# Product 4 of the second projection by two levels of Strassen in one core's fused attention and MLP kernel

## The chip, the cores and the metric

The kernel runs on one core of a Trainium2 chip. The metric is the device time of one execution in microseconds, lower is better. All arithmetic is in fp32. Engine names in the profile: PE is TensorE's matmul, PEld its weight load, DVE is VectorE, ACT is ScalarE, POOL is GpSimd, SP is SyncE, which here only issues DMAs.

## What is computed

The inputs are q, k, v of shape (8 batches, 8 heads, 576 tokens, 64), and two weight matrices. Cut to what matters:

```python
kv  = einsum('bhsd,bhse->bhde', k, v)
out = einsum('bhsd,bhde->bhse', q, kv)
x   = (out / sqrt(mean(out*out, -1) + 1e-6) * g_norm)   # -> (4608 tokens, 512)
h   = x @ w_in                                          # (4608, 512) @ (512, 2048)
g   = maximum(0.01 * h, h)
y   = g @ w_out                                         # (4608, 2048) @ (2048, 512)
```

Nearly all of the work is in the two projections h and y.

## The kernel before

**Blocks, chunks and slots.** The 4608 tokens are nine blocks of 512. Block 0 is done with plain matmuls. Blocks 1 to 8 (`i` in the main loop) go through the 2048 hidden features in four chunks (`c`) of 512. A running chunk number is `n = (i - 1) * 4 + c`, from 0 to 31. The main loop walks each chunk in seven slots, `t` = 0 to 6; `slot = 7 * c + t` counts within a block. In each slot the code writes out, in this order, one step of h, pieces of other work, and one step of the output product y. TensorE runs its instructions in that order. VectorE and GpSimd keep the written order too from block 2 on (`pin`), so a late instruction on one of these holds up whatever is written behind it.

**Strassen, one level and two.** Both projections use the Winograd form of Strassen's scheme: seven products of half-size matrices in place of eight. The products are numbered 1 to 7. One level of it for y gives products of 256 x 256 times 256 x 256 for a chunk: four pairs of 128 x 128 weights against 256 columns each, two TensorE instructions for each pair, so 8 instructions. From block 2 on, h is done by two levels (`product_h_two`): each of its seven products is split into seven quarters, and each quarter is one 128 x 128 by 128 x 128 matmul, which is 2 instructions.

**Where the results of y go.** Products 1, 6, 7, 4 of a chunk add up in one PSUM bank, and products 5 and 3 in another; the two banks `oa` and `oc` swap roles from chunk to chunk. After each product the bank as it stands is added to one quadrant of y in SBUF: 1 goes to "11", 5 and 1+6+7 to "22", 1+6 and 5+3 to "12", and 1+6+7+4 to "21". These additions are DVE instructions of 128 x 512, or ACT copies in the first chunk of a block (`done` in `product_o`). A quadrant leaves for DRAM after the last chunk of its block.

**Product 2 already goes by two levels.** For chunks 4 to 29, class `Second` does product 2 (the g12 part) as seven quarters. Its seven quarter products sit in the fourth column of the bank that holds the second group of the h quarters (`hb` or `hd`), one in each slot of chunk n + 2, and DVE adds each to the "11" quadrant with a 128 x 128 instruction. GpSimd makes the sums that these need: of the weights once (`inner_w2`), and of g12 per chunk (`inner_g`, four operations of 128 x 128, written at `t` = 4 and 6).

**Timing of the y products.** A queue runs two slots behind (`LAG = 2`): y's products of chunk n start at `t` = 2 of chunk n + 1. With product 2 elsewhere, the order is 1, 5, 6, nothing, 7, 3, 4, so that in the steady state the slots `t` = 0 to 6 hold, behind their eight h and `Second` quarters: product 3, product 4, product 1, product 5, product 6, nothing, product 7.

**What feeds and drains h.** For `t` = 0 to 6, h runs its products 1, 2, 6, 5, 7, 3, 4. Products 1, 6, 5, 4 are copied out of PSUM by ACT (line 951), 2, 7, 3 are added by DVE. At the end of the chunk seven DVE additions of 128 x 512 put the four quadrants of g together, ACT applies the leaky ReLU (`relu`, line 832) to each, and GpSimd makes four sums of them (`sums_of`) for y's products 3, 5, 6, 7.

**Other work.** Attention for a later batch is cut in steps placed by `FINE_SLOTS` and `LATE_SLOTS`. The Winograd sums of the next block's x are made on DVE in slots 20 to 22 (`sums`, from `sides_x`), and the two-level sums on GpSimd in slots 24, 25 and after the chunk (`inner`). The weight sums for y, `t12` and `t34`, are read back from DRAM for each chunk as two loads of 512 KB (`sides_w2`, line 673). The h weights are read through a ring of five.

Of the kernel before, what the change touches and what calls it, by code (L numbers as in the profile page):

```python
# [23 lines left out]
def kernel(  # L24
# [39 lines left out]
    P = 128  # L64
# [34 lines left out]
    NW = U * NE * P  # L99
    w1_all = consts.tile([P, 2 * NC * NW], F32, name="w1_all")  # L100
    stage = consts.tile([P, 3 * NW], F32, name="stage")
    pairs = consts.tile([P, 4 * NW], F32, name="pairs")
    g_all = [consts.tile([P, 4 * U * N2], F32, name=f"g_{i}") for i in range(2)]

    def view(t, lo, *shape):
# [79 lines left out]
    zeros = view(g_all[0], 0, NT)  # L185
    nc.vector.memset(zeros[:, :64], 0.0)
    nc.vector.memset(zeros[:, 64:], 0.0)
    ident = consts.tile([P, P], F32, name="ident")

    def make_ident():  # L190
        pin(nc.gpsimd.memset(ident, 1.0))
# [448 lines left out]
    def sides_w1(c):  # L640
# [9 lines left out]
        def more():  # L650
# [5 lines left out]

    w2_dram = [[dram.tile([P, 2, U, N2], F32, name=f"w2_{c}_{i}") for i in range(2)]
               for c in range(NC)]
    t12, t34 = pair(2, 2, U, N2), pair(3, 2, U, N2)
    writes = []  # L660

    def sides_w2(n):

        c = n % NC
        b11, b12 = w2_sb[0][c][:, :, :N2], w2_sb[0][c][:, :, N2:]
        b21, b22 = w2_sb[1][c][:, :, :N2], w2_sb[1][c][:, :, N2:]

        def sums(i):  # L670
            t = (t12, t34)[i]
            if n >= NC:
                pin(nc.sync.dma_start(t, w2_dram[c][i]))
                return
            if i == 0:
                add(nc.gpsimd, t[:, 0], b12, b11, True)
                add(nc.gpsimd, t[:, 1], b22, t[:, 0], True)
            else:
                add(nc.gpsimd, t[:, 0], b22, b12, True)
                add(nc.gpsimd, t[:, 1], b21, t12[:, 1], True)  # L680
            if (n, i) == (NC - 1, 1):

# [54 lines left out]
    def read(to):  # L737
        nonlocal n_read
        while n_read < min(to, len(reads)):
# [5 lines left out]
    qc = pair(0, 4, 3, P)  # L745
    xt1 = [work.tile([P, 2, N2], F32, tag="xt1", name="xt1"),
           view(w1_all, RING * NG + 24 * P, 2, N2)]
    xt24 = [work.tile([P, 2, 2, N2], F32, tag="xt24", name="xt24"),
            view(w1_all, RING * NG + 16 * P, 2, 2, N2)]
    xi = view(stage, 0, 3, 7, P)  # L750

    def sides_x(i):


        x = xTs.pop(i)
        b11, b12 = x[:, :2, :N2], x[:, :2, N2:]
        b21, b22 = x[:, 2:, :N2], x[:, 2:, N2:]
        home = i % 2 if i > 1 else 0
        t1, t2, t4 = xt1[home], xt24[home][:, 0], xt24[home][:, 1]
        if i == 1:  # L760
            t4 = opool.tile([P, 2, N2], F32, tag="o", name="xt4", bufs=6)
        t3 = b12
        sides = {1: b11, 2: b21, 3: b22, 4: t4, 5: t1, 6: t2, 7: t3}

        def sums():
            for t, a, b in ((t1, b12, b11), (t2, b22, t1), (t3, b22, b12), (t4, b21, t2)):
                add(nc.vector, t, a, b, True)
                yield

        batches, quarters, at = [], {k: {} for k in ORDER}, 0  # L770
        upper, lower = (x[:, h:h + 2, :].rearrange("p r (t v n) -> p t r v n", t=2, v=2)
                        for h in (0, 2))
        for js, y in (((1, 7), upper), ((2, 3), lower),
                      ((6, 4), xt24[home].rearrange("p t r (v n) -> p t r v n", v=2)),
                      ((5,), t1.rearrange("p r (v n) -> p r v n", v=2).unsqueeze(1))):
            terms = [y[:, :, r, v, :] for r in range(2) for v in range(2)]
            terms += [xi[:, k, at:at + len(js), :] for k in range(3)]
            batches.append(terms)
            for n, j in enumerate(js):
                for k, term in zip((1, 7, 2, 3, 5, 6, 4), terms):  # L780
                    quarters[k][j] = term[:, n, :]
            at += len(js)

        def inner(kind):
            for y11, y12, y21, y22, t1, t2, t4 in batches:
                if kind == 0:
                    add(nc.gpsimd, t1, y12, y11, True)
# [8 lines left out]
    def strassen(tags, left, right, done, order=ORDER, pieces=None):  # L796

# [3 lines left out]
        for i in order:  # L801

            if i is None:
                yield
                continue
            b = tags[0 if i in (1, 6, 7, 4) else 1]
            if i in FRESH:
                banks[b] = ps_m.tile([P, 2, N2], F32, tag=b, name=f"{b[0]}_{b[1]}")
            bank = banks[b]
            if pieces and b == tags[0]:  # L810
                if i == 1:
                    homes = [bank] + [ps_m.tile([P, 2, N2], F32, tag=t, name=f"o_{t}")
                                      for t in ("ha", "hc")]
                    ends = [t.rearrange("p u n -> p (u n)")[:, :cols.stop - cols.start]
                            for t, (_, cols) in zip(homes, pieces)]
                for to, (part, cols) in zip(ends, pieces):
                    for r in range(2):
                        matmul(to, lhsT=left(i, part, r), rhs=right(i, part, r)[:, cols],
                               start=(i == 1 and r == 0), stop=(r == 1), skip_group_check=True)
                done(i, ends)  # L820
                yield
                continue
            for part in range(2):
                for r in range(2):
                    matmul(bank[:, part, :], lhsT=left(i, part, r), rhs=right(i, part, r),
                           start=i in FRESH and part == 0 and r == 0, stop=(r == 1),
                           skip_group_check=True)
            done(i, bank.rearrange("p u (v n) -> p (u v) n", v=2))
            yield

# [47 lines left out]

    gi = view(pairs, 12 * P, 4, P)

    def inner_w2(c):
        y = w2_sb[1][c]
# [7 lines left out]

    def inner_g(c, half):

        g = g_of(c)[3]
        a11, a21, a12, a22 = (g[:, n, :] for n in range(4))
        s1, s2, s3, s4 = (gi[:, n, :] for n in range(4))
        if half == 0:
            add(nc.gpsimd, s1, a21, a22)
            add(nc.gpsimd, s2, s1, a11, True)  # L900
# [4 lines left out]
    class Second:  # L905
# [17 lines left out]
        def done(self, k, bank):  # L923
# [2 lines left out]
            add(nc.vector, to, bank, to)  # L926
            if self.n % NC == NC - 1 and k == ORDER[-1]:
                self.finish("11", self.o)

    def product_h_two(i, c, quarters, to, second):  # L930

# [41 lines left out]
    def product_o(n, g_sides, os, finish, second):  # L973

        c = n % NC
        w_sides, _ = sides_w2(n)
        sums = sides_w2(n + 1)[1] if n + 1 < NC * (NB - 1) else lambda i: None
        if c == 0:

            for key in ("12", "22", "11", "21"):  # L980
                os[key] = opool.tile([P, 2, N2], F32, tag="o", name=f"o{key}", bufs=6)
# [6 lines left out]

        def done(i, bank):
            key, fresh = into[i]  # L990
            if isinstance(bank, list):
                for at, (end, (part, cols)) in enumerate(zip(bank, pieces)):
                    to = os[key][:, part, cols]
# [8 lines left out]
                nc.scalar.copy(to, bank)  # L1002
            else:
                add(nc.vector, to, bank, to)
            if c == NC - 1 and i in (2, 7, 3, 4):
                finish(key, os[key])

            if i == (6 if second else 5):
                sums(0)
            elif i == 4:  # L1010
                sums(1)


        yield from strassen((("oa", "oc"), ("oc", "oa"))[n % 2], lambda i, part, r: g_sides[i][:, 2 * r + part, :],
                            lambda i, part, r: w_sides[i][:, r, :], done,
                           (1, 5, 6, None, 7, 3, 4) if second else ORDER,
                           pieces=pieces)

    def go(steps, n=None):
        while n is None or n > 0:  # L1020
# [16 lines left out]
    def first_block(between):  # L1037
# [26 lines left out]
                       start=(now[2] == 0), stop=(n == 2 * NC * U))  # L1064
            between(n, 1)
        for t in range(4):
            o = opool.tile([P, DM], F32, tag="o", name="o", bufs=6)
            if t % 2:
                nc.scalar.copy(o, accs[t])
            else:  # L1070
# [37 lines left out]
    for part in range(2):  # L1108
# [4 lines left out]
    FINE_SLOTS = {1: 1, 2: 1, 4: 1, 9: 1, 10: 2, 11: 1, 12: 1, 15: 1, 16: 2, 17: 2, 18: 1, 19: 1,  # L1113
                  23: 1, 24: 1, 25: 1, 26: 1}
    LATE_SLOTS = (3, 4)

    LAG = 2

# [1 line left out]
    HELD = (22, 24, 26)  # L1120
    o_queue, waited = collections.deque(), 0

    seconds = {}

    def second_of(n):
        if n in seconds:
# [9 lines left out]
    for i in range(1, NB):  # L1136
# [4 lines left out]
        for c in range(NC):  # L1141
# [3 lines left out]
            for t in range(7):  # L1145
                slot = 7 * c + t
                go(h_steps, 1)
                if not one:

                    if t == 6:  # L1150
                        go(h_steps, 1)
                    if slot in LATE_SLOTS:
                        go(late, 1)
                    for _ in range(FINE_SLOTS.get(slot, 0)):
                        go(a_steps, 1)
                    if i + 1 < NB:
                        if slot == 20:
                            x_sides, new_quarters, sums, inner = sides_x(i + 1)
                        if slot in (20, 21, 22):
                            go(sums, 2 if slot == 20 else 1)  # L1160
                        if slot == 24:
                            inner(0)
                        elif slot == 25:
                            inner(1)
                    load_some()

# [1 line left out]
                if now - 1 in seconds:  # L1168
# [2 lines left out]
                            inner_g((now - 1) % NC, half)  # L1171
                    if t == 5 and now <= 2 * NC:
                        inner_w2((now - 1) % NC)
                if slot == 4 and not one:
                    while writes:
                        pin(nc.sync.dma_start(*writes.pop()))
# [78 lines left out]
```

## Time and profile before

| | |
|---|---|
| time, median of 3 runs | 916.78 us (916.37 to 917.01) |
| span of the profiled run | 915.5 us |
| PEld, weight loads | 775.6 us, 85% |
| DVE | 628.2 us, 69% |
| ACT | 327.6 us, 36% |
| POOL | 367.0 us, 40% |
| DMA, all queues | 200.06 MB, mean 219 GB/s |

A group in the profile is one kind of instruction; its columns are the line, the engine, the operation, output and inputs with their shapes, the count, the busy time, the mean length of one, and the idle time of the engine just ahead of it with what ended that idle time. Line 118 is the helper through which every matmul goes, and line 636 the helper of every addition, so instructions are told apart by the tiles they name: `w` is a weight of y, `pairs` a buffer of weight sums and of other sums, `gs` the sums of g, `h_ha` to `h_hd` and `o_a`, `o_c` PSUM banks. The time of an instruction in the profile contains its latency, so matmuls in a row overlap: what one costs is the distance from its start to the next start.

In the timeline, chunks of 4 x about 24 us make a block of 96.8 us: product 1 of the third chunk of a block starts at 506.03 us in one block and at 602.92 us in the next.

### The profile page before, as it was taken

The page shows a single profiled execution, that of the slowest core. Times are in us where ns is not written, and L with a number is a line of the kernel's source. Part 1 is how long each engine was busy: PE and PEld are TensorE (multiplying, and loading weights), DVE is VectorE, ACT ScalarE, POOL GpSimd, SP SyncE. Part 2 cuts the span into 40 slices and gives each one's busy share as a digit, 9 for nine tenths or more (in the row PEclk, how much of TensorE's full clock was granted, in tenths as well). Part 3 has the DMA queues.
Part 4 walks back from the last instruction along what each step waited for, and adds up shares of the span by engine and source line. Part 5 has one row for each costly group of instructions (what it writes and reads, how often), then busy time and mean ns, then how long its engine had stood idle before and what let it go on. Part 6 is the DMA issues. An engine that isn't in the chain of part 4 may idle for free.

```text
span 915.5 us, 18030 instructions
## 1 busy us (share of the span) xinstructions
PE 909.1 (99%) x6976; PEld 775.6 (85%) x6976; DVE 628.2 (69%) x1168; ACT 327.6 (36%) x645; POOL 367.0 (40%) x440
## 2 busy tenths in 40 slices
PE   8999999999999999999999999999999999999998
PEld 5444448888998999899999999999999999999997
DVE  5876985587457876587756786678659755755565
ACT  5454533242135233533343324332343333223330
POOL 2000246977633472226321642264226422642222
DMA  9999908895599678877896689658765676667632
GB/s 267 243 243 237 239 35 258 263 304 167 175 360 286 224 213 263 235 233 211 255 261 216 219 250 263 230 179 227 224 184 176 188 221 200 184 187 223 199 107 92
DMA packets 90229, 200.06 MB, mean 219 GB/s; under 512 B 9888, under 2 KB 42272, under 8 KB 90144
## 3 DMA queue, kind: packets, MB, share of 16 engines
q1 hardware_dynamic: 79680, 187.04, 69.5%
q10 hardware_dynamic: 10016, 10.69, 3.4%
q8 instruction: 56, 0.92, 0.4%
q0 software_dynamic: 448, 1.18, 0.3%
q14 instruction: 29, 0.24, 0.1%
HBM read 172.39 MB, written 26.48 MB: 217 GB/s over the span
## 4 chain that ended last, share of the span: by engine, by line
PE 95%; DMA 2%; DVE 1%; POOL 1%; issue 0%; ACT 0%; ACTq 0%; DVEq 0%; POOLq 0%
PE o_a L118 18%; PE o_c L118 18%; PE h_ha L118 11%; PE h_hb L118 11%; PE h_hc L118 8%; PE h_hd L118 8%; PE o_acc L118 6%; PE h_ps L118 6%; PE o_ps L118 3%; PE h_a L118 1%; PE h_c L118 1%; PE kv_ps L118 1%; DMA pairs<-in_v_dram 1%; PE h_b L118 1%; PE h_d L118 1%; DMA w<-pairs 1%
## 5 line engine op out<-in xcount | busy, mean ns | idle before, releaser
L636 POOL TENSOR_TENSOR gs<-g 128x512 f32<-128x512 f32 x64 | 81.7, 1277 | 253.3 <-ACT g L832 253.3
L832 ACT ACTIVATE g<-g 128x512 f32<-128x512 f32 x124 | 78.2, 631 | 130.4 <-DVE g L636 130.4
L951 ACT COPY w_all<-h_ha 128x512 f32<-128x512 f32 x84 | 48.9, 582 | 173.9 <-PE h_ha L118 160.5
L118 PE MATMUL o_a<-pairs,gs 128*128 128x256 f32 x384 | 91.3, 381 | 0.0
L118 PE MATMUL o_c<-pairs,gs 128*128 128x256 f32 x376 | 89.2, 380 | 0.0
L636 DVE TENSOR_TENSOR o<-h_hb,o 128x128 f32<-128x128 f32 x104 | 29.8, 286 | 83.3 <-ACT pairs L951 83.2
L118 PEld LDWEIGHTS o_a<-pairs,gs 128*128 128x128 f32 x384 | 69.8, 190 | 9.2 <-POOL pairs L636 1.2
L636 DVE TENSOR_TENSOR o<-o_c,o 128x512 f32<-128x512 f32 (+1 forms) x91 | 61.1, 672 | 24.1 <-PE o_c L118 23.7
L118 PEld LDWEIGHTS o_c<-pairs,gs 128*128 128x128 f32 x376 | 68.3, 190 | 7.6
L636 DVE TENSOR_TENSOR o<-o_a,o 128x512 f32<-128x512 f32 x75 | 51.2, 682 | 28.2 <-PE o_a L118 28.1
L118 PE MATMUL h_ha<-stage,w_all 128*128 128x128 f32 x448 | 59.6, 276 | 0.0
L118 PEld LDWEIGHTS h_ha<-stage,w_all 128*128 128x128 f32 x448 | 56.6, 192 | 3.0 <-issue 0.7
L118 PE MATMUL h_ps<-xT,w_all 128*128 128x512 f32 (+1 forms) x136 | 58.1, 571 | 0.3 <-DVE w_all L258 0.3
L118 PE MATMUL o_acc<-w,g 128*128 128x512 f32 x128 | 57.7, 594 | 0.0
L636 DVE TENSOR_TENSOR g<-g,pairs 128x512 f32<-128x512 f32 x84 | 55.6, 689 | 1.9
L636 POOL TENSOR_TENSOR pairs<-g 128x128 f32<-128x128 f32 x52 | 23.7, 456 | 77.3 <-PE h_hb L118 48.5
L118 PEld LDWEIGHTS h_ps<-xT,w_all 128*128 128x128 f32 x136 | 25.4, 190 | 29.0 <-issue 26.1
L118 PEld LDWEIGHTS o_acc<-w,g 128*128 128x128 f32 x128 | 24.1, 190 | 30.2 <-issue 29.9
L636 DVE TENSOR_TENSOR w_all<-h_hc,w_all 128x512 f32<-128x512 f32 x56 | 38.3, 684 | 15.9 <-PE h_hc L118 15.6
L636 DVE TENSOR_TENSOR o<-h_hd,o 128x128 f32<-128x128 f32 x78 | 22.0, 283 | 38.2 <-ACT pairs L951 38.1
L118 PE MATMUL h_hb<-stage,w_all 128*128 128x128 f32 x336 | 46.7, 275 | 0.0
L636 POOL TENSOR_TENSOR pairs<-w 128x512 f32<-128x512 f32 x4 | 5.3, 1328 | 98.7 <-ACT cut L245 98.7
(229 smaller groups left out, 2262.4 us busy)
## 6 DMA issues: line engine op xcount, KB each, us to landing
w_all<-w SPq DMA_DIRECT2D x196, 448.0 KB, 4.2
pairs<-w SPq DMA_DIRECT2D x56, 512.0 KB, 4.3
out_dram<-o ACTq DMA_DIRECT2D x35, 256.0 KB, 4.4
v_in<-in_v_dram SPq DMA_DIRECT2D x29, 288.0 KB, 5.5
k_in<-in_k_dram SPq DMA_DIRECT2D x28, 288.0 KB, 5.3
q_in<-in_q_dram SPq DMA_DIRECT2D x56, 144.0 KB, 6.0
q_in<-in_q_dram SPq DMA_DIRECT2D x56, 140.0 KB, 6.0
w<-stage SPq DMA_DIRECT2D x12, 512.0 KB, 4.8
```

Of the source, the lines that this page charges most:

```text
L118: pin(nc.tensor.matmul(*args, **kw))
L636: ins = eng.tensor_tensor(out_, a, b_, op=ALU.subtract if minus else ALU.add)
L832: nc.scalar.activation(t, t if src is None else src, func=AF.Prelu, alpha=SLOPE)
L951: nc.scalar.copy(q[:, at], bank)
```

## The change

Product 4 (g22 times a weight sum, into the quadrant "21") goes by two levels as well, for chunks 8 to 28, which are 21 chunks. The aim is fewer TensorE columns: seven quarters in place of four matmuls of twice the width.

- The class `Fourth` runs the seven quarters in four steps: quarters 1, 2, 5 behind h at `t` = 1 of chunk n + 2; 6 and 3 at `t` = 2, behind the next chunk's product 1; 7 behind h at `t` = 3; 4 behind h at `t` = 4. They use the bank in which products 1, 6, 7 of chunk n stood, in three columns: 1, 6, 7, 4 in the first, 2 in the second, 5 and 3 in the third. Each quarter is added to "21" by its own instruction of 128 x 128.
- Product 7 can then not flow on into product 4 in the bank. The sum 1+6+7 goes into a new tile "7", which is added to "22" and to "21" at the end of each block.
- The order of y's products becomes 1, nothing, 6, 5, 7, 3, nothing.
- GpSimd makes the inner sums for g22 and g12 in one go: `inner_g` keeps four operations, now 128 x 256. The inner sums of the weights are made once, in block 2 (`inner_w4`), and stored in DRAM; they are read back per chunk with seven quarters in place of four.
- The x sums move from slots 20, 21, 22 to slots 22, 24, 25, 26, and the inner x sums from slots 24 and 25 to slot 27.
- Room is found: `ident` shares a tile with `xt24`, `pairs` grows by 512 columns, and the output tiles are split in two tags.

```diff
+    def four(n):
+        return 2 * NC <= n < NC * (NB - 1) - 3
...
+            if n >= NC and i:
+                if row != 1:
+                    pin(nc.sync.dma_start(t[:, 0], w2_dram[c][i][:, 0]))
+                if row == 0:
+                    return
+                if not four(n):
+                    pin(nc.sync.dma_start(t[:, 1], w2_dram[c][i][:, 1]))
+                    return
+                pin(nc.sync.dma_start(f4, w4_dram[c][:, :4, :]))
+                pin(nc.sync.dma_start(f4_more, w4_dram[c][:, 4:, :]))
+                return
...
+            if behind and i == 1:
+                behind()
             done(i, bank.rearrange("p u (v n) -> p (u v) n", v=2))
...
-        g = g_of(c)[3]
-        a11, a21, a12, a22 = (g[:, n, :] for n in range(4))
-        s1, s2, s3, s4 = (gi[:, n, :] for n in range(4))
+        g = view(g_all[c % 2], 0, 4, 4, P)
+        a11, a21, a12, a22 = (g[:, n, 2:, :] for n in range(4))
+        s1, s2, s3, s4 = (gi_two[:, :, n * P:n * P + P] for n in range(4))
...
+    class Fourth:
+        STEPS = (1, 2, 5), (6, 3), (7,), (4,)
+        COLUMN = {1: 0, 6: 0, 7: 0, 4: 0, 2: 1, 5: 2, 3: 2}
...
+        def step(self, at):
+            if at == 0:
+                self.bank = ps_m.tile([P, 4, P], F32, tag=self.tag, name=f"f_{self.tag}")
+            for k in self.STEPS[at]:
+                matmul(self.bank[:, self.COLUMN[k], :], lhsT=self.left[k], rhs=self.right[k],
+                       start=(k == 1), stop=True, skip_group_check=True)
+            for k in self.STEPS[at]:
+                bank = self.bank[:, self.COLUMN[k], :]
+                v, s = INTO[k]
+                to = self.o_of("21")[:, v, s * P:s * P + P]
+                if self.n % NC == 0 and k in (1, 5, 6, 4):
+                    nc.scalar.copy(to, bank)
+                else:
+                    add(nc.vector, to, bank, to)
+            if at == 3:
+                self.last()
...
+            if fourth and i == 7:
+                if c == NC - 1 or not four(n + 1):
+                    add(nc.vector, os["22"], os["22"], os["7"])
...
+        if fourth or four(n - 1):
+            order = (1, None, 6, 5, 7, 3, None if fourth else 4)
+        elif second:
+            order = (1, 5, 6, None, 7, 3, 4)
...
+    FOURTH_AT = {1: 0, 3: 2, 4: 3}
...
+                    if t in FOURTH_AT and four((i - 1) * NC + c - 2):
+                        fourths[(i - 1) * NC + c - 2].step(FOURTH_AT[t])
...
-                        if slot in (20, 21, 22):
-                            go(sums, 2 if slot == 20 else 1)
-                        if slot == 24:
+                        if slot in (22, 24, 25, 26):
+                            go(sums, 1)
+                        if slot == 27:
                             inner(0)
-                        elif slot == 25:
                             inner(1)
```

More of the change, by code (lines that the diff above doesn't have):

```diff
@@ L101 @@
     stage = consts.tile([P, 3 * NW], F32, name="stage")
-    pairs = consts.tile([P, 4 * NW], F32, name="pairs")
+    pairs = consts.tile([P, 4 * NW + 4 * P], F32, name="pairs")
     g_all = [consts.tile([P, 4 * U * N2], F32, name=f"g_{i}") for i in range(2)]
@@ L187 @@
     nc.vector.memset(zeros[:, 64:], 0.0)
-    ident = consts.tile([P, P], F32, name="ident")
+    xt24_home = work.tile([P, 2, 2, N2], F32, tag="xt24", name="xt24")
+    ident = xt24_home[:, 0, 0, :P]
     def make_ident():
@@ L658 @@
                for c in range(NC)]
-    t12, t34 = pair(2, 2, U, N2), pair(3, 2, U, N2)
+    w4_dram = [dram.tile([P, 7, P], F32, name=f"w4_{c}") for c in range(NC)]
+    t12, t34 = pair(2, 2, U, N2), view(pairs, 28 * P, 2, U, N2)
+    f4 = t34[:, 1].rearrange("p u (v n) -> p (u v) n", v=2)
+    f4_more = view(stage, 21 * P, 3, P)
+    def four(n):
+        return 2 * NC <= n < NC * (NB - 1) - 3
     writes = []
@@ L668, in sides_w2, with sums @@
         b21, b22 = w2_sb[1][c][:, :, :N2], w2_sb[1][c][:, :, N2:]
-        def sums(i):
+        def sums(i, row=None):
             t = (t12, t34)[i]
+            if n >= NC and i:
[9 more added lines that the diff above has]
+                return
             if n >= NC:
@@ L747 @@
            view(w1_all, RING * NG + 24 * P, 2, N2)]
-    xt24 = [work.tile([P, 2, 2, N2], F32, tag="xt24", name="xt24"),
+    xt24 = [xt24_home,
             view(w1_all, RING * NG + 16 * P, 2, 2, N2)]
@@ L760, in sides_x @@
         if i == 1:
-            t4 = opool.tile([P, 2, N2], F32, tag="o", name="xt4", bufs=6)
+            t4 = opool.tile([P, 2, N2], F32, tag="o11", name="xt4", bufs=2)
         t3 = b12
@@ L794, in sides_x, with strassen @@
         return sides, quarters, sums(), inner
-    def strassen(tags, left, right, done, order=ORDER, pieces=None):
+    def strassen(tags, left, right, done, order=ORDER, pieces=None, behind=None):
         banks = {}
@@ L876, in product_h, with inner_w4 @@
         sums_of(c, to)
-    gi = view(pairs, 12 * P, 4, P)
+    gi_two = pairs[:, 12 * P:].rearrange("p (a n) -> p a n", a=2)
+    gi_four, gi = (gi_two[:, a, :4 * P].rearrange("p (k n) -> p k n", k=4) for a in range(2))
+    def inner_w4():
+        y11, y12, y21, y22 = (f4[:, k, :] for k in range(4))
+        t1, t3, t2 = (f4_more[:, k, :] for k in range(3))
+        add(nc.gpsimd, t1, y12, y11, True)
+        add(nc.gpsimd, t3, y22, y12, True)
+        add(nc.gpsimd, t2, y22, t1, True)
+        add(nc.gpsimd, y12, y21, t2, True)
     def inner_w2(c):
@@ L928, in done, with __init__ @@
                 self.finish("11", self.o)
+    class Fourth:
+        STEPS = (1, 2, 5), (6, 3), (7,), (4,)
+        COLUMN = {1: 0, 6: 0, 7: 0, 4: 0, 2: 1, 5: 2, 3: 2}
+        def __init__(self, n, tag, o_of, last):
+            self.n, self.tag, self.o_of, self.last = n, tag, o_of, last
+            g = g_of(n % NC)[2]
+            self.left = {1: g[:, 0, :], 2: g[:, 2, :], 4: g[:, 3, :],
+                         **{k: gi_four[:, at, :] for at, k in enumerate((5, 6, 7, 3))}}
+            self.right = {**{k: f4[:, at, :] for at, k in enumerate((1, 4, 2, 3))},
+                          **{k: f4_more[:, at, :] for at, k in enumerate((5, 7, 6))}}
+        def step(self, at):
[14 more added lines that the diff above has]
+                self.last()
     def product_h_two(i, c, quarters, to, second):
@@ L976, in product_o, with o_of @@
         w_sides, _ = sides_w2(n)
-        sums = sides_w2(n + 1)[1] if n + 1 < NC * (NB - 1) else lambda i: None
+        sums = sides_w2(n + 1)[1] if n + 1 < NC * (NB - 1) else lambda i, row=None: None
+        fourth = four(n)
+        def o_of(key):
+            if c == 0 and key not in os:
+                home = {"tag": "o11", "bufs": 2} if key == "11" else {"tag": "o", "bufs": 4}
+                os[key] = opool.tile([P, 2, N2], F32, name=f"o{key}", **home)
+            return os[key]
         if c == 0:
-            for key in ("12", "22", "11", "21"):
-                os[key] = opool.tile([P, 2, N2], F32, tag="o", name=f"o{key}", bufs=6)
+            o_of("11")
         pieces = ((0, slice(0, N2)), (1, slice(0, P)), (1, slice(P, N2))) \
@@ L990, in done @@
             key, fresh = into[i]
+            if fourth and i == 7:
+                key, fresh = "7", True
+            o_of(key)
             if isinstance(bank, list):
@@ L1004, in done, with last @@
                 add(nc.vector, to, bank, to)
-            if c == NC - 1 and i in (2, 7, 3, 4):
+            if i == 7 and NC <= n:
+                sums(1, 0)
+            if fourth and i == 7:
+                if c == NC - 1 or not four(n + 1):
+                    add(nc.vector, os["22"], os["22"], os["7"])
+                if c == NC - 1:
+                    finish("22", os["22"])
+            elif c == NC - 1 and i in (2, 7, 3, 4):
                 finish(key, os[key])
-            if i == (6 if second else 5):
+            if i == (6 if second else 5) if order[1] is not None else i == 5:
                 sums(0)
-            elif i == 4:
[L1011 to L1017, printed above, removed]
+            elif i == 4 and NC <= n < 2 * NC:
+                inner_w4()
+                later.extend(([3, lambda: (
+                    pin(nc.sync.dma_start(w4_dram[c][:, :4, :], f4)),
+                    pin(nc.sync.dma_start(w4_dram[c][:, 4:, :], f4_more)))],
+                    [4, lambda: sums(1, 1)]))
+            elif i == 4:
+                sums(1, 1 if NC <= n else None)
+        def last():
+            sums(1, 1)
+            if c == NC - 1 or not four(n + 1):
+                add(nc.vector, os["21"], os["21"], os["7"])
+            if c == NC - 1:
+                finish("21", os["21"])
+        tags = (("oa", "oc"), ("oc", "oa"))[n % 2]
+        order = ORDER
+        if fourth or four(n - 1):
+            order = (1, None, 6, 5, 7, 3, None if fourth else 4)
+        elif second:
+            order = (1, 5, 6, None, 7, 3, 4)
+        if fourth:
+            fourths[n] = Fourth(n, tags[0], o_of, last)
+        yield from strassen(tags, lambda i, part, r: g_sides[i][:, 2 * r + part, :],
+                            lambda i, part, r: w_sides[i][:, r, :], done, order, pieces=pieces,
+                            behind=(lambda: fourths[n - 1].step(1)) if four(n - 1) else None)
+    fourths = {}
     def go(steps, n=None):
@@ L1066, in first_block @@
         for t in range(4):
-            o = opool.tile([P, DM], F32, tag="o", name="o", bufs=6)
+            o = opool.tile([P, DM], F32, tag="o", name="o", bufs=4)
             if t % 2:
@@ L1121 @@
     o_queue, waited = collections.deque(), 0
-    seconds = {}
+    seconds, later = {}, []
     def second_of(n):
@@ L1173 @@
                         inner_w2((now - 1) % NC)
+                for job in list(later):
+                    job[0] -= 1
+                    if job[0] == 0:
+                        job[1]()
+                        later.remove(job)
                 if slot == 4 and not one:
```

## The prediction

> **What bounds the kernel.** I read the page from its first part (busy time) to its fourth (the chain that ended last), then the groups kept apart by shape, then TensorE's waits, then one timeline.
>
> ```profile
> PE 909.1 (99%) x6976; PEld 775.6 (85%) x6976; DVE 628.2 (69%) x1168; ACT 327.6 (36%) x645; POOL 367.0 (40%) x440
> ...
> PE 95%; DMA 2%; DVE 1%; POOL 1%; issue 0%; ACT 0%; ACTq 0%; DVEq 0%; POOLq 0%
> ```
>
> TensorE is 99% busy and 95% of the chain. In the list of waits, TensorE has no row at all from 280 us on: in the blocks that change nothing makes it wait, and every microsecond it saves is a microsecond of the kernel, as long as no new wait appears.
>
> ```profile
> L118 PE MATMUL o_c<-pairs,g 128*128 128x256 f32 x124 | 29.4, 379 | 0.0
> L118 PE MATMUL h_hb<-w,pairs 128*128 128x128 f32 x104 | 20.1, 275 | 0.0
> L636 DVE TENSOR_TENSOR o<-o_a,o 128x512 f32<-128x512 f32 x75 | 51.2, 682 | 28.2 <-PE o_a L118 28.1
> L636 DVE TENSOR_TENSOR o<-h_hb,o 128x128 f32<-128x128 f32 x104 | 29.8, 286 | 83.3 <-ACT pairs L951 83.2
> ```
>
> The first row is product 4 as it is now, the second a quarter product of the kind that takes its place; no idle time stands before either. The third is the DVE addition that empties a bank, the fourth that of a quarter: a quarter of the data costs 286 ns against 682. The wait in the fourth row matters below: the quarter's addition waits for an ACT copy out of the same bank.
>
> The timeline from the end of one chunk to `t` = 3 of the next (start, length, instruction):
>
> ```profile
> 518.46 1.89 PE L118 MATMUL o_a<-pairs,gs 128*128 128x256 f32 x8
> 519.64 0.29 DVE L636 TENSOR_TENSOR o<-h_hb,o 128x128 f32<-128x128 f32 x1 [1.80 <-ACT pairs L951]
> 519.85 0.68 DVE L636 TENSOR_TENSOR g<-w_all 128x512 f32<-128x512 f32 x1
> ...
> 525.21 0.63 ACT L832 ACTIVATE g<-g 128x512 f32<-128x512 f32 x1 [0.42 <-DVE g L636]
> ...
> 525.49 1.89 PE L118 MATMUL o_a<-pairs,g 128*128 128x256 f32 x8
> 525.75 0.46 ACT L951 COPY pairs<-h_hb 128x384 f32<-128x384 f32 x1
> ...
> 526.24 0.29 DVE L636 TENSOR_TENSOR o<-h_hb,o 128x128 f32<-128x128 f32 x1 [1.06 <-ACT pairs L951]
> ...
> 527.22 1.05 PE L118 MATMUL h_ha<-stage,w_all 128*128 128x128 f32 x8
> ...
> 528.11 0.28 DVE L636 TENSOR_TENSOR o<-h_hd,o 128x128 f32<-128x128 f32 x1
> 528.11 0.83 PE L118 MATMUL h_hb<-stage,w_all 128*128 128x128 f32 x6
> ...
> 529.00 1.89 PE L118 MATMUL o_c<-w,g 128*128 128x256 f32 x8
> ```
>
> Product 4 starts at 525.49 and the next h at 527.22: **1.73 us**. Eight quarter instructions run from 527.22 to 528.11, so a quarter product of two is **0.222 us**.
>
> **What the Trainium skill says.** "Perfetto Trace Analysis", section Identifying the Most-Contended Engine, calls matmul busy time no good measure and takes the busy share of weight loads: that is 93% here (92.8 us of the 100 from 420 us on), so TensorE is the bound by that measure too. "TensorE: Matmul & The Clock Gate", section Back-to-back issue gap, gives 134 cycles for 128 columns and 262 for 256: two of the small cost 2% more than one of the large. The trace has 111 and 216 ns, 3% more, so the narrow matmuls give back a little of what they save. "PSUM — Partial Sum Buffer", section PSUM bank collisions raise a hardware error, says that two engines must be kept off one bank at a time even in different columns; the ACT wait in the fourth group row is that rule at work, and I apply it to `Fourth`'s bank. "Perfetto Trace Analysis", section Optimizing Scalar/DVE Operations, names a fixed overhead per instruction; 286 against 682 ns agrees.
>
> **The change, part by part.**
>
> *TensorE.* Per chunk 8 instructions (1.73 us) go and 7 quarters come: 7 x 0.222 = 1.554 us. Saved: 0.176 us. Over 21 chunks **3.70 us**. This lies wholly on the path. Swapping product 5 and the empty slot moves work and adds none.
>
> *DVE.* Per chunk seven quarter additions for one of 0.68: 7 x 0.286 - 0.68 = +1.32 us; in a first chunk ACT takes four of them and the first fill of "7", and a last chunk has two more additions of 0.68. Per block some 5.5 us (3 x 1.32 + 0.86 - 0.68 + 1.37) on 69 to 70 busy in 97: DVE goes from 72% to 77%. It isn't the bound as a sum; what counts is whether it is late at a join.
>
> *ACT.* Four small copies and one large for one large, once a block: about 1.3 us of 61 idle. Hidden.
>
> *POOL.* `inner_g`: four operations at 0.73 (the rows of 128 x 256) for 0.455: +1.1 us per chunk. It idles 7.35 us before each chunk's first g sum, waiting for ACT. Hidden. `inner_w4`: 4 x 0.46 in four chunks of block 2, behind the g sums: hidden in the same idle time.
>
> *DMA.* 192 KB more per chunk (448 for 256), 4 MB in all on 200; median landing of the weight sums 4.3 us, and the issue at `t` = 4 has four slots, some 12 us, until `t` = 1. Hidden. In block 2 the store of the new sums sits in SP's queue ahead of the h weights and may hold them a slot or two; the ring is five deep. Zero, bound 1 us.
>
> *The x sums.* The inner sums in slot 27 are 12 POOL operations, 8.1 us (508.8 to 516.8 in the trace with their gaps). They can start once DVE has made the sums (slots 25, 26), and are done early in slot 28; the first quarters that need them run in slot 30, and the g sums behind them could not start before the end of slot 29 anyway. Zero. On DVE the move takes three additions (0.68, 0.68, 1.28 us) away from the crowded end of chunk 2.
>
> *The new waits.* Four joins, on the boundary shown:
>
> 1. The second bank of h's product 6. Behind that bank's matmuls wait product 1 and all of TensorE. DVE's g additions, the last ReLU, the ACT copy of `h_hb` and the `Second` addition at 526.24 must be over first: they end at 526.53, 8.07 us after h's product 4 ended (518.46). TensorE has 9.65 us for this now (to 528.11). With product 4 cut to three quarters, 0.67 us, it has 8.58: slack 0.5. At the next boundary the added "22" sum takes 0.7 of 0.9. No wait, but tight.
> 2. Quarters 6 and 3 need the additions of 1, 2, 5. DVE is through with `Second` at 528.3 and then needs about 0.7: 529.0. TensorE reaches them at 527.94 + 1.73 = 529.67. Slack 0.6. Product 1 behind h is what hides this.
> 3. Quarter 7 needs the additions of 6 and 3. TensorE is there 1.78 us (eight h quarters) after quarter 3, at 531.9. Ahead of those additions DVE has attention's work for `t` = 1 and 2: two transposes of 1.25 and 1.23 us and one `Second` addition, so 529.1 + 2.7 = 531.7, and the additions end at 532.2: a wait of 0.3 us. This is where the change pays. It happens once a block where attention has transposes in slots 1 and 2 (blocks 4, 5, 6): 0.9 us at most. In a first chunk the additions of one bank alternate between ACT and DVE; I put 0 to 0.5 us on that, six times, and take 0.05.
> 4. Quarter 4 needs the addition of 7, and has 1.78 us for about 1.1. Product 5 then needs the bank, 3.5 us later. No wait.
>
> Taken: 0.9 + 0.3 = 1.2 us, less what an earlier wait gives DVE at a later join; say **1.0 us**. Sum: 916.78 - 3.70 + 1.0 = 914.1; I say **914.0**.
>
> **Rivals.**
>
> *Waits eat most of it (no change).* If join 2 or 3 is late by 0.15 us in each of 21 chunks, 3.2 us go: 916.8. For it: three of four slacks are under 0.7 us, and ACT's order isn't pinned. Against it: three boundaries in four have lighter attention work than the one shown. It covers 915 to 918.6.
>
> *A wait takes the place of the width (slower).* If ACT is held by DVE in the shared bank, and `Second`'s addition comes 0.8 us later, join 1 breaks by 0.3 us at each boundary and join 3 by the same: 21 x 0.6 = 12.6 less 3.7 gives 925.7; with join 1 alone, 21 x 0.3 = 6.3 gives **919.4**, which I take. For it: 83 us of such waits already stand before the quarter additions. Against it: they end on time now, and product 5 in the once empty slot gives ACT's attention work 1.73 us more ahead of the boundary.
>
> *POOL is late at the block boundary (slower).* The inner sums, put late, push the g sums back: six times 2 us, 916.78 - 3.70 + 12 = 925. Against it: the 7.35 us of idle time.
>
> **How the numbers follow.** 0.68 for the forecast (912.9, no wait at all, to 914.9), 0.15 for no change, 0.14 for the second and 0.03 for the third rival. The fastest possible is 916.78 - 3.70 = 913.1, less 0.3 of scatter: low end 912.8. The high end takes in the second case and the slow side up to 918.8, and leaves out some 0.15. Faster by over 0.2% is below 914.95: 0.68; slower is above 918.6: 0.17; between: 0.15.
>
> **What would show it.** TensorE's instruction count up by 21 x 6 = 126, its starts at 111 and 216 ns as now. A block of 96.8 us becomes 96.1 plus the waits. TensorE's waits should show rows of `f_oa` or `f_oc` behind DVE, around 1 us in all, mostly at quarter 7. Rows of `h_hb` or `h_hd` behind DVE or ACT speak for the second rival, rows behind POOL for the third. DVE near 77% in the middle blocks. I am wrong if TensorE waits over 1.9 us in all, or if the quarters' starts are further apart than 111 ns.

## The result, and the profile after

The changed kernel takes **926.26 us** (median of 4 runs, 925.04 to 928.04) against 916.71 for the kernel before on the same chips: ratio 1.0106, 95% interval 1.0088 to 1.0124. It is slower by 9.6 us, where 2.8 less were forecast, and the time lies above the range of 912.8 to 918.8. Lines of the page of the changed kernel, busy times and chain:

```profile
PE 908.9 (98%) x7102; PEld 778.0 (84%) x7102; DVE 660.9 (72%) x1282; ACT 332.7 (36%) x669; POOL 423.7 (46%) x456
...
PE 85%; DVE 7%; DMA 4%; ACT 2%; issue 1%; POOL 1%; SPq 0%; DVEq 0%; ACTq 0%; POOLq 0%
```

TensorE has the 126 instructions more that were forecast, but its share of the chain fell from 95% to 85%, and DVE has 7%. TensorE's list of waits, without rows from 280 us on before, now has these (total us, times, longest):

```profile
PE h_hb L118 <- DVE o L637: 7.4, 6, 2.1
...
PE f_oa L118 <- DVE o L637: 0.7, 2, 0.3
PE f_oa L118 <- DMA pairs<-w: 0.5, 1, 0.5
```

The large row is the second bank of h's product 6, in slot 2 (join 1 of the prediction), six times: once at each of the six boundaries into blocks 3 to 8, and at no other chunk boundary. The timeline around one of them (start, length, instruction; x2 and x3 are neighbours shown as one):

```profile
521.61 1.24 POOL L637 TENSOR_TENSOR stage<-w_all,stage 128x256 f32<-128x256 f32 x1
522.18 1.22 DVE L637 TENSOR_TENSOR g<-w_all,pairs 128x512 f32<-128x512 f32 x1
...
523.32 0.68 DVE L637 TENSOR_TENSOR o<-o_a,o 128x512 f32<-128x512 f32 x1
...
523.92 2.01 DVE L637 TENSOR_TENSOR g<-g,w_all 128x512 f32<-128x512 f32 x2
...
524.21 2.31 POOL L637 TENSOR_TENSOR xT<-xT 128x256 f32<-128x256 f32 x2
...
525.96 3.10 DVE L637 TENSOR_TENSOR g<-g,pairs 128x512 f32<-128x512 f32 x3
...
529.10 0.63 ACT L853 ACTIVATE g<-g 128x512 f32<-128x512 f32 x1 [1.37 <-DVE g L637]
...
529.64 0.46 ACT L1013 COPY pairs<-h_hb 128x384 f32<-128x384 f32 x1
...
530.13 0.29 DVE L637 TENSOR_TENSOR o<-h_hb,o 128x128 f32<-128x128 f32 x1 [1.06 <-ACT pairs L1013]
...
530.48 0.94 PE L118 MATMUL h_hb<-stage,w_all 128*128 128x128 f32 x6 [1.06 <-DVE o L637]
```

Read the lengths. DVE's additions of g took 0.68 us each before. Here the first still does; the six others take 0.83 to 1.22 us, 1.06 on average. GpSimd's inner x sums of 128 x 256 beside them, 0.73 before, take 0.9 to 1.24. Yet DVE's addition out of the PSUM bank `o_a`, in the middle of the same stretch, keeps its 0.68. From the first addition of g to the end of the last it takes 7.5 us, with 5.33 at the same boundary before. The last ReLU, the copy out of `h_hb`, the `Second` addition and TensorE are all behind that, in the order of the prediction's join 1.

So the suspect is not `Fourth` at all but the move that came with it: the inner x sums, from slots 24 and 25 to slot 27, now run beside DVE's additions of g, and push the last operations of `inner_g` in among them as well. That is **theory A**. **Theory B**, nearest to the prediction's second rival: the quarter additions make DVE late wherever the inner sums run.

The profile before already held such a pair, and the prediction passed over it. The x sums that it lists as "0.68, 0.68, 1.28 us" are additions of one size, each of two SBUF tiles. From the kernel before:

```profile
496.26 0.69 DVE L636 TENSOR_TENSOR w_all<-xT,w_all 128x512 f32<-128x512 f32 x1
...
502.27 1.28 DVE L636 TENSOR_TENSOR xT<-xT 128x512 f32<-128x512 f32 x1
...
503.08 1.62 POOL L636 TENSOR_TENSOR gs<-gs,g 128x512 f32<-128x512 f32 x1
...
505.34 1.15 DVE L636 TENSOR_TENSOR w_all<-xT,w_all 128x512 f32<-128x512 f32 x1
...
505.89 1.73 POOL L636 TENSOR_TENSOR gs<-g,gs 128x512 f32<-128x512 f32 x1
```

The two long ones run beside GpSimd's sums of g, the short one while GpSimd rests. In the change, the sum that took 1.28 us runs while GpSimd rests, and takes 0.68 (at 516.73). So 1.28 us was not the operation's own length but a collision's.

### The profile page after: what moved, and what is told of

It reads as the page before. It is cut to its first block, busy times and chain, and to the rows that moved or that the text cites. A ratio compares the mean times of both kernels' runs of the same rounds, so it can differ in the third digit from the quotient of the medians.

```text
span 924.1 us, 18530 instructions
## 1 busy us (share of the span) xinstructions
PE 908.9 (98%) x7102; PEld 778.0 (84%) x7102; DVE 660.9 (72%) x1282; ACT 332.7 (36%) x669; POOL 423.7 (46%) x456
## 4 chain that ended last, share of the span: by engine, by line
PE 85%; DVE 7%; DMA 4%; ACT 2%; issue 1%; POOL 1%; SPq 0%; DVEq 0%; ACTq 0%; POOLq 0%
PE o_a L118 14%; PE o_c L118 14%; PE h_ha L118 9%; PE h_hb L118 9%; PE h_hc L118 7%; PE h_hd L118 7%; PE o_acc L118 6%; PE h_ps L118 6%; DVE g L637 4%; PE o_ps L118 3%; PE f_oc L118 2%; PE f_oa L118 1%; PE h_a L118 1%; PE h_c L118 1%; DMA w<-pairs 1%; DVE o L637 1%
## 5 line engine op out<-in xcount | busy, mean ns | idle before, releaser
L637 DVE TENSOR_TENSOR o<-o_c,o 128x512 f32<-128x512 f32 (+1 forms) x81 | 54.3, 671 | 20.1 <-PE o_c L118 19.9
L637 POOL TENSOR_TENSOR pairs<-g 128x256 f32<-128x256 f32 x52 | 42.1, 810 | 50.4 <-PE h_hd L118 35.4
L637 DVE TENSOR_TENSOR g<-g,pairs 128x512 f32<-128x512 f32 x84 | 62.1, 766 | 1.9
L637 DVE TENSOR_TENSOR o<-o_a,o 128x512 f32<-128x512 f32 x64 | 43.7, 683 | 23.4 <-PE o_a L118 23.3
L118 PEld LDWEIGHTS h_hb<-stage,w_all 128*128 128x128 f32 x336 | 42.1, 192 | 8.6 <-DVE o L637 8.6
L1013 ACT COPY pairs<-h_hb 128x384 f32<-128x384 f32 x84 | 39.8, 474 | 17.3 <-PE h_hb L118 15.9
```

Of the source, the lines that this page charges most:

```text
L118: pin(nc.tensor.matmul(*args, **kw))
L637: ins = eng.tensor_tensor(out_, a, b_, op=ALU.subtract if minus else ALU.add)
L1013: nc.scalar.copy(q[:, at], bank)
```

## The experiments

The time up to block 3 varies from run to run with the first loads: the profiled executions reach the start of product 1 that stands at 312.25 us before anywhere between 311.2 and 325.0 us. So beside the measured time the table gives the **stretch** from that start to the last start of matmuls of that kind (901.81 us before), in the profiled execution: 589.56 us before, 598.47 after. Each run of an experiment was timed beside the kernel before on one chip; the third column has that time.

| kernel | time, us | beside it, before | ratio, 95% interval | stretch against before, us |
|---|---|---|---|---|
| the change | 926.26 | 916.71 | 1.0106 (1.0088 to 1.0124) | +8.91 |
| e1_old_slots | 925.80 | 917.33 | 1.0089 (1.0074 to 1.0104) | +6.95 |
| e2_move_alone | 920.44 | 917.33 | 1.0032 (1.0020 to 1.0044) | +2.98 |
| e3_inner_25 | 923.58 | 917.33 | 1.0060 (1.0044 to 1.0076) | +4.93 |
| e4_no_inner | 915.00 | 917.33 | 0.9971 (0.9960 to 0.9982) | -3.03 |
| e5_split_inner | 915.33 | 917.03 | 0.9992 (0.9973 to 1.0010) | -0.57 |
| e5_again | 915.99 | 917.28 | 0.9991 (0.9980 to 1.0003) | -0.76 |
| e6_inner1_late | 920.43 | 917.03 | 1.0041 (1.0024 to 1.0057) | +1.97 |
| e7_before_no_inner | 917.08 | 917.03 | 1.0003 (0.9988 to 1.0017) | +0.01 |
| e8_split_fine | 929.02 | 917.03 | 1.0119 (1.0095 to 1.0144) | +2.24 |
| e9_fine_from_4 | 914.84 | 917.28 | 0.9970 (0.9959 to 0.9981) | -3.32 |

**The sums left out, and the control.**

```diff
-                        if slot == 27:
+                        if slot == 27 and i == 1:
                             inner(0)
                             inner(1)
```

> The change with the first two inner x steps (12 GpSimd operations a block) left out from block 2 on, so that part of the x quarters is not computed; nothing else moves. Theory A: additions of g 5.3 us, no waits in slot 2, 913.3 to 914.5 us: the price of the collision alone, 11 to 13 us. Theory B: 922 to 926 us.

> A control: the kernel before with the same twelve GpSimd operations a block left out (from block 2 on part of the x quarters is not computed). In the kernel before they run beside other work and meet no addition of g, so every theory expects the time of the kernel before, 916.3 to 917.3 us; if it falls, leaving work out gains in itself and the change without these operations proves less.

Without these sums the change takes 915.0 us, half a microsecond above the forecast of theory A. Its additions of g take 5.26 us at every block boundary, and from 280 us on one wait of 0.3 us, at quarter 7, is left in TensorE's list. The last three additions of g at the boundary shown above:

```profile
520.86 2.02 DVE L637 TENSOR_TENSOR g<-g,pairs 128x512 f32<-128x512 f32 x3
```

The same operations left out of the kernel before gain nothing (1.0003). So leaving out work isn't the gain: in the stretch, the inner sums in slot 27 cost the change 8.91 + 3.03 = 11.9 us, and `Fourth` with the x sums in their new slots brings 3.0. From product 1 to product 1, 9.2 of the 11.9 us stand at the six block boundaries, 1.9 in the three chunks behind these that have a wait at quarter 7 or a slow clock (last section), and 0.8 around the first load of `Fourth`'s weight sums. Theory B is out as the main cause: all of `Fourth`'s additions are in this kernel.

**The move alone.** The two places that the diff of the change shows last, put into the kernel before.

> The kernel before with only the x sums (slots 22, 24, 25, 26) and the inner x sums (slot 27) moved; no Fourth. Theory A: the additions of g at the block boundary take 7.5 us here too, but TensorE still has the whole product 4 in slot 1 (9.65 us in place of 8.58), so h's product 6 waits only some 0.4 us at each of six boundaries: 917.5 to 920 us. Theory B: no change, 916.5 to 917.

920.44 us, half a microsecond above the forecast of theory A and far from that of theory B. The additions of g at the block boundaries take 7.3 to 7.7 us here too, with no `Fourth` in the kernel, and TensorE waits at join 1:

```profile
524.34 3.10 DVE L636 TENSOR_TENSOR g<-g,pairs 128x512 f32<-128x512 f32 x3
...
PE h_hb L118 <- DVE o L636: 1.8, 4, 0.8
```

The whole move costs 3.0 us by itself; with `Fourth`, its inner sums cost 11.9. What `Fourth` takes out of slot 1 (1.07 us, four matmul pairs for three quarters) was the slack in which the stretched additions could still hide for the most part: the waits of `h_hb` grow from 1.8 us here to 7.4 in the change, 5.6 us more, and five boundaries with `Fourth` at 1.07 us make 5.4. That is a sum that fits, not a test: boundary by boundary the growth is 0.6 to 2.1 us.

**The disputed operations by themselves.** Twenty DVE additions of 128 x 512 and eighteen or twenty GpSimd additions of 128 x 256, nothing else.

> Nothing of the reference is computed: only the disputed operations, one after the other and side by side. Twenty DVE additions of 128x512 out of two SBUF tiles alone, twenty GpSimd additions of 128x256 alone, then both together; then DVE additions of a PSUM bank and an SBUF tile alone, and with GpSimd. Theory A (two SBUF inputs share a port with GpSimd): 0.68 us and 0.73 us alone, together 1.1 to 1.2 us each, as in slot 27; with a PSUM input DVE keeps 0.68 us. If the stretching in the change came from anything else (order, dependencies, DMA), both keep their time side by side.

The timeline, one row per batch:

```profile
6.81 12.13 DVE L83 TENSOR_TENSOR dve_o<-dve_a,dve_b 128x512 f32<-128x512 f32 x20
...
20.05 13.88 POOL L87 TENSOR_TENSOR pool_o<-pool_a,pool_b 128x256 f32<-128x256 f32 x20
...
35.05 20.16 POOL L87 TENSOR_TENSOR pool_o<-pool_a,pool_b 128x256 f32<-128x256 f32 x18
35.47 21.49 DVE L83 TENSOR_TENSOR dve_o<-dve_a,dve_b 128x512 f32<-128x512 f32 x20
...
58.56 12.05 DVE L83 TENSOR_TENSOR dve_o<-bank,dve_b 128x512 f32<-128x512 f32 x20
...
71.61 12.56 POOL L87 TENSOR_TENSOR pool_o<-pool_a,pool_b 128x256 f32<-128x256 f32 x18
72.02 12.05 DVE L83 TENSOR_TENSOR dve_o<-bank,dve_b 128x512 f32<-128x512 f32 x20
```

Divide each length by its count. With both inputs in SBUF, DVE takes 0.61 us for each alone and 1.07 beside GpSimd (its last two run after GpSimd has ended); GpSimd 0.69 alone and 1.12 beside DVE. With one input in PSUM, DVE takes 0.60 alone and 0.60 beside GpSimd, which takes 0.70. So of these pairs the two hinder each other only where DVE reads two SBUF tiles. "SBUF — State Buffer", section Who interferes with whom, of the Trainium skill says just that: a DVE instruction with two SBUF inputs contends with a GpSimd instruction that reads SBUF, because its second input comes through the shared read interface. Here, while both run, each starts a new addition every 1.13 us, less than the 1.30 that the two need in turn, so a part of the two lengths does overlap.

**A smaller dose.** The change with only the four operations of `inner(1)` moved, behind the second sum of g.

> A smaller dose: the change with only inner(1), four of the twelve GpSimd operations of slot 27, moved behind the second sum of g. Theory A: GpSimd overlaps the additions of g for some 5 us in place of 7.6, these take 6.5 to 7 us, and h_hb waits some 0.3 to 0.8 us less at each boundary: 2 to 5 us under the change, 920 to 924 us. Theory B: as the change, 925 to 927.

920.43 us, within theory A's range of times; the gain over the change, 6.9 us in the stretch, is above the 2 to 5 forecast. At five of the six boundaries GpSimd is busy for 3.9 to 4.8 us while g is added, and the additions take 6.6 to 6.8 us from first to last in place of 7.5 to 7.8; at the sixth boundary the two figures are 2.4 and 5.8. The waits of `h_hb` fall from 7.4 to 2.4 us.

**The move undone.** Back to slots 20, 20, 21, 22 for the x sums and 24, 25 for the inner ones.

> The change with one part undone: the x sums go back to slots 20, 20, 21, 22 and the inner x sums to slots 24 and 25. Theory A (GpSimd's inner sums, now at the block boundary, share SBUF with the seven DVE additions of g and stretch them from 5.3 to 7.5 us, so that h's product 6 waits in slot 2): the additions of g at the block boundary take 5.3 us again and the waits there (7.4 us in all) go; in their place chunk 2's boundary, which gets two x sums back, waits some 0.4 us a block; 915 to 916.5 us. Theory B (DVE is late because Fourth gives it seven small additions a chunk, wherever the inner sums are): the waits stay, 923 to 926 us.

925.8 us: a miss for theory A's number, and inside theory B's range. What theory A says of the block boundary holds all the same: the additions of g are back at 5.26 us from block 4 on, and no wait stands there. The loss has moved to the boundary into the fourth chunk: `h_hb` waits there, as forecast, for less than 0.4 us a block, but quarter 7 in slot 24, which I had given no wait, costs 1.2 to 2.2 us. The timeline of one:

```profile
509.74 1.66 DVE L637 TENSOR_TENSOR w_all<-xT,w_all 128x512 f32<-128x512 f32 x1
...
512.28 1.56 DVE L373 TENSOR_TENSOR sum<-sum,sq 128x384 f32<-128x384 f32 x2 [0.42 <-ACT sq L369]
513.77 0.60 DVE L637 TENSOR_TENSOR o<-f_oc,o 128x128 f32<-128x128 f32 x2
...
514.43 0.49 PE L118 MATMUL f_oc<-stage,pairs 128*128 128x128 f32 x2 [1.00 <-DVE o L637]
```

DVE comes to the additions of quarters 6 and 3 (513.77) late: ahead of them stand an x sum of 1.66 us (GpSimd's sums of g run beside it) and attention's sums, of which the second takes 1.09 us, where the first takes 0.56, beside the inner x sums that begin at 512.39. This is read from the timeline; no run tests it alone. So the move was not idle: it freed this boundary, and paid at the other. With `Fourth` in place the old slots are hardly better: 2.0 us of the stretch.

**Earlier, all at once.** x sums in slots 22, 22, 24, 24, and both inner steps in slot 25.

> The change with the x sums in slots 22 and 24 (two each) and both inner steps in slot 25 instead of 27, so that GpSimd is through before the additions of g begin. Theory A: additions of g 5.3 to 5.7 us at every boundary, waits of TensorE of 1 us in all, at quarter 7: 913.5 to 915 us, faster than both kernels. Theory B: 923 to 926 us.

923.58 us: a miss. The additions of g are still stretched (7.4 us from the first start to the last end at the boundary after 520 us). Two x sums in slot 22 meet GpSimd's sums of g and take 1.31 and 1.64 us; the third x sum is done at 515.8 and the last at 516.4; GpSimd sits idle for 6.16 us, starts the inner sums only at 515.91, and then still has `inner_g`, written behind them, to run until 529. I had looked at where the work is written and not at when its inputs are ready.

**Split, and kept clear.** Two of the four batches of `inner(0)` in slot 24, those that need no late x sum, and two in slot 26; x sums in slots 22, 24, 24, 25; `inner(1)` between the second and third sum of g.

```diff
-                        if slot in (22, 24, 25, 26):
-                            go(sums, 1)
-                        if slot == 27:
-                            inner(0)
-                            inner(1)
+                        if slot in (22, 24, 25):
+                            go(sums, 2 if slot == 24 else 1)
+                        if slot == 24:
+                            inner(0, (1, 3))
+                        if slot == 26:
+                            inner(0, (0, 2))
+                            between_sums.append(lambda: inner(1))
```

> The change with GpSimd's inner x sums kept out of the stretch in which DVE adds g together: two of the four batches in slot 24 and two in slot 26 (x sums in slots 22, 24, 24, 25), and the third term (12.. the four subtractions of inner(1)) between the second and third sum of g. All the work is done. Theory A: additions of g 5.3 us at the block boundary, no wait of h_hb there; TensorE waits 1 to 2 us in all at quarter 7; 914 to 915.5 us. Theory B (late DVE from Fourth's additions): 922 us or more. Theory C (any shift of the inner sums only moves the collision, as with slot 25): waits of over 4 us turn up elsewhere, 918 us or more.

> e5_split_inner again, beside e9_fine_from_4 and the kernel before on one chip: 914.5 to 915.5 us, some 0.2% under the kernel before.

915.33 and, on another chip, 915.99 us: the first within its forecast, the second half a microsecond above. All the work is done, the `h_hb` row is gone from the waits, and 9.5 us of the stretch with it. Neither interval lies wholly below 1, so this is no proven gain over the kernel before. What is left in the two lists from 280 us on are quarter 7 (0.5 us in all) and the first load of `Fourth`'s weight sums (1.5 and 1.3 us). Both profiled executions (917.51 and 919.68 us) are slower than the median of their runs, so the typical run may have less of the latter.

**The wait at quarter 7.** As e5_split_inner, one attention step moved out of slot 2; first in all blocks, then from block 4 on, which is the edit shown.

```diff
+    FINE_LATER = {**FINE_SLOTS, 2: 0, 5: 1}
...
-                    for _ in range(FINE_SLOTS.get(slot, 0)):
+                    for _ in range((FINE_LATER if i > 3 else FINE_SLOTS).get(slot, 0)):
```

> As e5_split_inner, and attention's steps of slots 2 and 4 moved to slots 4 and 5, so that DVE has one transpose fewer ahead of the additions of quarters 6 and 3. If the wait at quarter 7 in slot 3 is made by the transposes, as the prediction has it, the waits of f_oa (0.5 us a block in three blocks) go, and the time is 0.5 to 1.5 us under e5_split_inner: 913 to 914.5 us.

> e5_split_inner with one attention step moved from slot 2 to slot 5, from block 4 on only, so that the loads of the earlier blocks keep their order. If the transposes in slots 1 and 2 make the wait at quarter 7 in slot 3, the f_oa waits behind DVE in blocks 4 to 6 (some 0.45, 0.6 us each) go, and from the third product 1 of block 3 to the end it takes some 1 us less than e5_split_inner; 913.5 to 915 us, faster than the kernel before by 0.2 to 0.35%. If late DVE comes from elsewhere they stay, and the time is that of e5_split_inner.

In all blocks the time is 929.0 us, where 913 to 914.5 were forecast. TensorE waits 8.0 us for the loads of v, in two places before 280 us, and 3.9 for weight sums in block 3. In the code, attention's steps also queue the later loads, which fits; from the product 1 that starts at 382.17 us before to the end it takes 2.3 us less than the kernel before. From block 4 on only, it takes **914.84 us**, ratio 0.9970 (0.9959 to 0.9981): faster than both kernels. From 280 us on TensorE's list has no row: the waits behind DVE are gone, and so is the wait for the first weight sums, which this edit doesn't touch. From the product 1 that starts at 382.17 us before to the end, where the edit acts, it takes 1.0 us less than e5_split_inner, as forecast; the other 1.8 us stand at that load. The timeline at the block boundary:

```profile
518.76 0.73 POOL L637 TENSOR_TENSOR pairs<-g,pairs 128x256 f32<-128x256 f32 x1
...
520.74 0.69 DVE L637 TENSOR_TENSOR g<-w_all,pairs 128x512 f32<-128x512 f32 x1
...
521.95 1.41 DVE L637 TENSOR_TENSOR g<-g,w_all 128x512 f32<-128x512 f32 x2
523.39 2.02 DVE L637 TENSOR_TENSOR g<-g,pairs 128x512 f32<-128x512 f32 x3
...
526.15 1.27 POOL L637 TENSOR_TENSOR gs<-g 128x512 f32<-128x512 f32 x1 [6.66 <-ACT g L853]
```

GpSimd ends at 519.5 and starts again at 526.15; in between the additions of g run at 0.68.

## Why the prediction was wrong

- **The step that failed** is the sentence on the x sums: "Zero". It asked only whether GpSimd would be done in time for the quarters that need its sums, and it was. It did not ask what GpSimd's running does to DVE in that stretch, though the 1.28 us that it reads for one x sum is the same collision. The term, set at 0, is 11.9 us in the presence of `Fourth`, 9.2 of them at join 1.
- **Join 1**: the chain and its order were right, and its slack nearly so: in e9_fine_from_4 the `Second` addition ends at 526.76 us and the matmuls behind it start at 527.09, 0.3 us against 0.5. At the ordinary chunk boundaries no wait came. It broke at block boundaries only, since the additions of g in it grew by 2.2 us. The second rival had the right join with the wrong cause (ACT held in the shared bank) and the wrong count (21 times). The third rival had GpSimd at the block boundary, but as a late g sum; nothing waits for those. That two sums under these rivals, 925.7 and 925, come near the measured time is chance.
- **TensorE's saving** was right: where nothing disturbs, a chunk takes 22.70 us from product 1 to product 1 (750.97 to 773.67) for 22.87 before (743.23 to 766.10), 0.17 us against 0.176, at the pitches of 111 and 216 ns. e4_no_inner and e9_fine_from_4 show 3.0 and 3.3 us of the 3.70 in the stretch.
- **Join 3**: right in place, and roughly in size: starts at quarter 7 stand 0.6 us apart in blocks 4 and 5 for the usual 0.11, 0.5 us against 0.3 forecast. With one transpose moved away from it (e9_fine_from_4) it is gone. In how many blocks it comes depends on how late DVE already is: in one, block 6, without the inner sums (e4_no_inner), in three in e6_inner1_late.
- **DVE's load**: 76% in a block (74.85 of 98 us), 77% forecast.
- **DMA**, set at zero with a bound of 1 us: 0.5 us in the list of the change, at the first step of `Fourth` alone; 1.3 to 1.5 in the two profiles of the split kernel, none in those of e4_no_inner and e9_fine_from_4. Why it comes and goes was not settled.

## What to carry to other kernels

An operation moved off one engine's crowded stretch still has to be held against what the other engines run in its new place: the length that the profile before shows for it is that of its old place and its old neighbours. Look there for instructions of one form whose length varies along the trace, as the x sums' did (0.69 and 1.15 us); where DVE adds two SBUF tiles while GpSimd reads SBUF, price both at the longer figure. And a shorter TensorE slot is also a shorter cover: a narrower product that gains 3.0 us and a move that costs 3.0 us, each by itself, can share one slack and break it together.

## What was not expected of the hardware

After one of the waits of the change, of about 2 us, TensorE ran on at half its clock for some 3 us. In the table of windows PEclk is the figure behind POOL's busy time:

```profile
625.00:630.00 5.00, 3.17 (x29) 2.98 (x28) 3.90 (x6) 3.16 (x6) 4.84 (x5) 1.00 0.33 100
630.00:633.00 3.00, 3.00 (x12) 2.55 (x11) 2.97 (x8) 0.48 (x1) 2.92 (x4) 0.50 0.45 123
```

The matmuls of product 1 there start 427 ns apart for the usual 216, which adds some 1.5 us to the wait. That pause had starts 2.11 us apart. A longer one in the next block (2.37 us apart, at 724.9 us) had no such tail, while in e8_split_fine the clock fell to half at each of three waits of 3.5 to 4.5 us. So a wait of 2 us may cost more than its length, but not each time.
